# W3 and W_out by casting transfers from GpSimd, and a new order of the first steps, in a fused retention and FFN kernel

## The chip, the cores and the metric

The kernel runs on one core of a Trainium2 chip. The metric is the device time of one launch in microseconds (us). The profile gives one execution, in which the engines are called PE (TensorE, matmuls), PEld (its weight loads), DVE (VectorE), ACT (ScalarE), POOL (GpSimd) and SP (SyncE); the queues that issue transfers carry a q behind the name, so SPq is SyncE's queue. All transfers are carried out by the core's 16 DMA engines.

## What is computed

The reference first runs a retention recurrence for each batch and head and then a multiplicative FFN over all tokens:

```python
gamma = 1.0 - 2.0 ** (-5.0 - arange(8))
for t in range(768):                                  # q, k, v: 4 x 8 x 768 x 64
    state = gamma * state + outer(k[t], v[t])         # per batch and head, 64 x 64
    y[t] = q[t] @ state / sqrt(64)
x = y.transpose(0, 2, 1, 3).reshape(3072, 512)
a = x @ w1; b = x @ w2                                # w1, w2: 512 x 1024
out = ((a * b) @ w3) @ w_out                          # w3: 1024 x 1024, w_out: 1024 x 512
```

All inputs and the output are fp32 in DRAM. The kernel computes in fp16 with fp32 sums.

## The kernel before

The 3072 tokens are worked through as 12 tiles of 256, three for each batch. For one tile the steps are: load q, k, v (`load`, line 79), convert them to fp16 (`cast`, `cast_v`), turn q and k so that the head dimension lies on the partitions (`turn` and `turned`, or `dma_turn`), make masked scores (`scores`, `mask`), the tile's contribution to the state (`kv`, `state`), the part of the output that comes from the state and the part within the tile (`inter` in two parts, with `fence`, a small ACT copy, between them, then `av`), and write the result x as fp16 (`x_out`). Then follow the FFN's products with W1 and W2 and the product with the last matrix. For tiles 0 and 1 the W1 and W2 products go in steps of one 128-row block of a weight (`rows(W, tile, half, block)`, line 619 for the matmul), so that a step can start when its block is there. Later tiles use Strassen-like combinations of the weights (`combine`, `sums`, `prod`, line 867 for the matmul).

W3 and W_out are multiplied once, at the start: the product W3O = W3 W_out, 1024 x 512, takes the place of the two last matrices. W3 has eight blocks of 128 rows. For each block f the steps are: load it (`fetch('r5')` loads block 5 through `load_rows`, line 97, into an fp32 staging tile), convert it to fp16 (`cast_w3` or `cast_w3_half`, on DVE, ACT or POOL), turn it with eight 128x128 transposes on PE (`turn_w3`, matmul at line 260; half turns at line 249), copy the turned block from PSUM (`turned_w3`), and multiply it with the four parts of W_out (`w3_mm(f, i)`, four matmuls of 256 columns at line 280); when all four parts are done, `w3_out` copies the sum to SBUF. W_out comes in four parts of 256 rows (`fetch('wo2')` through `load_wo`, line 102), each converted by `cast_wo` (line 230). `fetch('w10')` loads block 0 of W1, `fetch('k0')` tile 0 of k.

Staging tiles are 16 in number (`NSTAGE`), 512 KB each, used in turn by all loads. All loads are issued by SP, in the order of the `fetch` lines, and in the trace their data come in that order. `warm(m)` runs m matmuls of 512 columns on zeros (line 796); they compute nothing that is used. POOL makes the constant tables: `identity()` (needed by the turns), `numbers`, `late_numbers`, `keeps` and `step_decays`.

The order of all steps is written out by hand as one long list, from line 948 to the end of the function; each engine works through its own instructions strictly in that order. Around the change the list reads, in the kernel before: loads of blocks 5, 2, 1, W_out 2, block 4, W_out 3, 0, 1, blocks 3, 6, 7, then tokens k0, q0, v0, block 0, tokens q1, k1, v1, then W1 and W2.

## Time and profile before

| | us |
|---|---|
| median of three runs (175.75 to 176.5) | 175.91 |
| the profiled execution, whole time | 176.04 |
| its span, first to last instruction | 174.2 |
| PE busy | 166.7 |
| PEld busy | 135.9 |
| DVE busy | 129.0 |
| ACT busy | 97.9 |
| POOL busy | 84.8 |

Queue q1, which holds all loads and stores of SP, carried 39.33 MB; 29.36 MB were read from DRAM and 6.29 MB written.

How to read the profile: a row of the timeline gives the start, the duration, the engine, the line of the kernel, the operation, output and input by the program's names with shape and type, how many instructions are merged into the row, and in brackets the idle time of the engine before it and what ended it. A row of the chain of waits gives the start, the length and what the time is put down to; the chain is followed back from the last instruction, at each step to what released it. PE's busy time is modelled, since matmuls are pipelined. Matmuls, copies and table work count as busy; issuing a transfer does not.

### The profile page before, as it was taken

Reading aid. Unit: us, or ns where it says so; the run is one execution under the profiler, and the core shown is the slowest. Engines: PE = TensorE matmul, PEld = TensorE weight load, DVE = VectorE, ACT = ScalarE, POOL = GpSimd, SP = SyncE. Lnnn points to the kernel's source line nnn. Section 1 sums busy time; section 2 is a strip of 40 time slices with the busy share of each in tenths; the row PEclk is TensorE's granted clock in tenths of the full one; section 3 lists DMA queues with packets and bytes.
Section 4 is the critical chain, followed back from the end, with each engine's and each line's share of the span. In section 5 each row is a group of like instructions: output and inputs, shape, how many; then the busy total and the mean of one; then the engine's idle time right before and its main releaser. Section 6 shows DMA issues by size and latency. Waiting matters only on the chain.

```text
span 174.2 us, 7288 instructions
## 1 busy us (share of the span) xinstructions
PE 166.7 (96%) x3196; PEld 135.9 (78%) x3196; DVE 129.0 (74%) x240; ACT 97.9 (56%) x169; POOL 84.8 (49%) x106
## 2 busy tenths in 40 slices
PE   6779999999999999999999999999999999999992
PEld 2349988778976799597899977959999598695972
DVE  0372469887865769979989698786998949686690
ACT  2055669688745596490653655637465483552732
POOL 1541841742899587496485966887312062000000
DMA  5999999999999999999978999999999999120033
GB/s 194 378 412 397 298 323 230 393 416 328 253 205 230 248 180 236 191 143 249 162 180 181 148 286 172 223 217 192 183 208 211 276 413 384 43 103 4 0 126 120
DMA packets 76160, 39.80 MB, mean 228 GB/s; under 512 B 53088, under 2 KB 71776, under 8 KB 76128
## 3 DMA queue, kind: packets, MB, share of 16 engines
q1 hardware_dynamic: 76128, 39.33, 92.8%
q8 instruction: 25, 0.41, 1.0%
q14 instruction: 7, 0.06, 0.1%
HBM read 29.36 MB, written 6.29 MB: 205 GB/s over the span
## 4 chain that ended last, share of the span: by engine, by line
PE 91%; DMA 3%; ACT 2%; SPq 0%; issue 0%; DVE 0%; ACTq 0%
PE psF L867 26%; PE psF L641 9%; PE psX L641 8%; PE psK L867 5%; PE psX L867 5%; PE psS L641 5%; PE psF L280 4%; DMA st<-in_moe_w_dram 3%; PE psF L619 3%; PE psX L509 3%; PE psX L280 2%; PE psS L619 2%; PE psF L653 2%; PE psX L535 2%; PE psS L396 2%; PE psK L619 1%
## 5 line engine op out<-in xcount | busy, mean ns | idle before, releaser
L867 PEld LDWEIGHTS <-wt 128*128 128x128 f16 x640 | 37.5, 98 | 0.5
L641 PEld LDWEIGHTS <-ht 128*128 128x128 f16 x224 | 21.0, 98 | 14.5 <-DVE ht L66 0.2
L867 PEld LDWEIGHTS <-w 128*128 128x128 f16 x480 | 28.8, 98 | 1.8
L63 ACT COPY u<-psF 128x512 f32<-128x512 f32 x32 | 18.4, 589 | 8.7 <-PE psF L867 6.4
L66 POOL TENSOR_TENSOR c<-u,p 128x512 f32<-128x512 f32 x12 | 15.2, 1276 | 11.7 <-ACT u L63 10.5
L867 PE MATMUL psF<-sodd,wt 128*128 128x128 f16 x240 | 18.1, 219 | 0.0
L641 PE MATMUL psF<-w3o,ht 128*128 128x256 f16 (+1 forms) x96 | 17.1, 326 | 0.0
L641 PE MATMUL psX<-w3o,ht 128*128 128x512 f16 (+1 forms) x80 | 15.2, 336 | 0.0
L66 DVE TENSOR_TENSOR ht<-psF,c 128x512 f16<-128x512 f32 x20 | 13.6, 687 | 0.9 <-POOL c L66 0.4
L619 PEld LDWEIGHTS <-w 128*128 128x128 f16 x128 | 12.3, 98 | 2.1 <-issue 0.4
L66 DVE TENSOR_TENSOR ht<-psX,c 128x512 f16<-128x512 f32 x19 | 12.8, 687 | 0.8 <-PE psX L867 0.4
L280 PEld LDWEIGHTS <-w3t 128*128 128x128 f16 x128 | 11.8, 98 | 2.1 <-DVE w3t L63 0.6
L66 POOL TENSOR_TENSOR v<-st,VN 128x1024 f16<-128x1024 f32 x6 | 11.4, 1902 | 1.3 <-DMA st<-in_v_dram 0.7
L874 ACT COPY psX<-psF 128x512 f32<-128x512 f32 x19 | 10.4, 576 | 2.4 <-issue 1.2
L413 DVE TENSOR_TENSOR am<-psS,keep 128x512 f16<-128x512 f32 x17 | 11.5, 684 | 0.3 <-PE psX L396 0.2
L867 PE MATMUL psX<-xt,w 128*128 128x128 f16 x152 | 11.6, 219 | 0.0
L867 PE MATMUL psF<-seven,wt 128*128 128x128 f16 x160 | 11.4, 219 | 0.0
L66 POOL TENSOR_TENSOR q<-st,QS 128x1024 f16<-128x1024 f32 x5 | 10.7, 2140 | 1.2 <-DMA st<-in_q_dram 1.2
L672 ACT ACTIVATE osb<-psF 128x512 f32<-128x512 f32 x8 | 4.8, 598 | 11.6 <-PE psF L641 11.6
L867 PE MATMUL psF<-xt,wt 128*128 128x128 f16 x160 | 11.1, 219 | 0.0
L867 PE MATMUL psF<-xt,w 128*128 128x128 f16 x160 | 11.1, 219 | 0.0
L66 DVE TENSOR_TENSOR c<-psK,u 128x512 f32<-128x512 f32 x10 | 6.9, 692 | 5.0 <-PE psK L867 4.4
(167 smaller groups left out, 375.0 us busy)
## 6 DMA issues: line engine op xcount, KB each, us to landing
st<-in_moe_w_dram SPq DMA_DIRECT2D x16, 512.0 KB, 7.9
st<-in_q_dram SPq DMA_DIRECT2D x12, 512.0 KB, 5.8
st<-in_v_dram SPq DMA_DIRECT2D x18, 256.0 KB, 5.9
st<-in_k_dram SPq DMA_DIRECT2D x18, 256.0 KB, 5.8
out_dram<-osb SPq DMA_DIRECT2D x9, 512.0 KB, 6.4
st<-in_moe_w_out_dram SPq DMA_DIRECT2D x4, 512.0 KB, 8.9
st<-in_k_dram SPq DMA_DIRECT2D x3, 512.0 KB, 10.8
st<-in_v_dram SPq DMA_DIRECT2D x3, 512.0 KB, 8.8
```

The lines of the kernel that those rows point to most:

```text
L63: {"v": nc.vector.tensor_copy, "g": nc.gpsimd.tensor_copy, "s": nc.scalar.copy}[eng](dst, src)
L66: (nc.vector if eng == "v" else nc.gpsimd).tensor_tensor(dst, a, b, op)
L280: nc.tensor.matmul(acc[f][:, cols], lhsT=w3t[f][:, g * 128 : (g + 1) * 128], rhs=WO[i][:, r, cols], start=(first and (r, c) == (0, 0)), st ...
L396: nc.tensor.matmul(ps[r][half(g), a, s, :], lhsT=kT[n][half(r), s, a, half(g)], rhs=qchunk(n, r, a, s, g), start=(a == 0 and s == 0), stop ...
L413: nc.vector.tensor_tensor(t[:, :, :, :].rearrange("p a s i -> p (a s) i"), ps[:, :, :, :].rearrange("p a s i -> p (a s) i"), keep64[:, :]. ...
L509: nc.tensor.matmul(dst, lhsT=TS[n, c][half(r), a, :], rhs=rhs, start=((g, o) not in begun), stop=False, skip_group_check=True,)
L535: nc.tensor.matmul(o, lhsT=v16[n][half(g), t, h * D : (h + 1) * D], rhs=rhs, start=((g, c) not in begun), stop=(n >= EO or t == 1), skip_g ...
L619: nc.tensor.matmul(rows_ps[w, n, uh][j // 2][:, j % 2, :], lhsT=W[d][:, f * 128 : (f + 1) * 128], rhs=XT[n][:, :, d, :], start=(first and ...
L641: nc.tensor.matmul(ps[:, x * w : (x + 1) * w], lhsT=HT[n][:, tb, f, :], rhs=W3O_all[:, f, c0 + x * w : c0 + (x + 1) * w], start=(f == 0 an ...
L672: nc.scalar.activation(o_tile(n, tb)[:, c0:c1], o_ps.pop((n, tb, c0, c1))[:, :], AF.Copy, scale=final_scale)
L867: nc.tensor.matmul(ps[:, j, :], lhsT=lhsT, rhs=rhs, start=(opens and j == 0 and c == 0), stop=(i in (2, 3, 4) and j == 3 and c == 1), skip ...
L874: nc.scalar.copy(WB[n, u, "C"][:, :, :], WB[n, u, "A"][:, :, :])
```

## The change

Seven row blocks of W3 (all but block 0) and all four parts of W_out no longer come through fp32 staging tiles and a conversion on an engine. GpSimd issues a transfer for each, from fp32 in DRAM straight into the fp16 tile (`gw3`, `gwo`), and the transfer converts. A new step `hold(f)` has SP issue a copy of 16 numbers out of the fp16 block f; SP waits for that block's transfer before it can issue this, and all token loads stand behind it in SP's list. Block 0 and W1 and W2 still come from SP into staging tiles and are converted on the engines (a function `gw` for W1 and W2 by casting transfer is added and is called nowhere).

The list of steps is written anew from its start to about line 1160 (tiles 0 to 2), and from there on steps are moved by one or a few places among their neighbours. Blocks are worked in the order 4, 1, 5, 2, 3, 7, 6, 0 by full turns; conversions of W1 and W2 go to other engines (POOL and DVE take more of them); the first W1 rows are those of block 2, and `fence(1)` stands ahead of the W1 conversions on ACT; the first loads after the tokens are W1 blocks 0, 2, 1, 3.

The diff up to the first W1 rows; the rest of it moves steps only.

```diff
@@ -186,6 +186,7 @@
     col_f = const.tile([128, 2, 128], FP, name="col_f")
     pos_f = const.tile([128, 2, 2, 64], FP, name="pos_f")
 
+    hold_t = const.tile([1, 16], HP, name="hold_t")
     W1 = [wpool.tile([128, DFF], HP, name=f"w1_{i}") for i in range(4)]
     W2 = [wpool.tile([128, DFF], HP, name=f"w2_{i}") for i in range(4)]
     WO = [wpool.tile([128, 2, DM], HP, name=f"wo_{i}") for i in range(4)]
@@ -226,6 +227,27 @@
 
     w3h, w3p, w3t, acc, w3n = {}, {}, {}, {}, {}
     w3h_tags = []
+
+    def gwo(i):
+        nc.gpsimd.dma_start(
+            WO[i][:, :, :], moe_w_out[i * 256 : (i + 1) * 256, :].rearrange("(p t) n -> p t n", t=2)
+        )
+
+    def gw3(f):
+        w3h[f] = att.tile([128, 1024], HP, tag="kq"[len(w3h_tags) % 2] + "16", name="w3h", bufs=3)
+        w3h_tags.append(f)
+        nc.gpsimd.dma_start(w3h[f][:, :], moe_w3[f * 128 : (f + 1) * 128, :])
+
+    def hold(f):
+        nc.sync.dma_start(hold_t[:, :], w3h[f][0:1, 0:16])
...
-    fetch('r5')
+    gw3(5)
+    warm(2, 'F2')
+    gw3(4)
+    gw3(1)
+    warm(3, 'F2')
+    gwo(3)
+    gwo(0)
     identity()
-    fetch('r2')
-    warm(2, 'F2')
-    fetch('r1')
+    step_decays()
+    gwo(2)
+    turn_w3(4, 'S0')
+    keeps()
+    warm(8, 'X1')
+    turned_w3(4, 's')
+    gw3(2)
+    gwo(1)
+    turn_w3(1, 'F0')
+    gw3(3)
+    turn_w3(5, 'K')
+    late_numbers()
+    turned_w3(1, 's')
     warm(3, 'F2')
-    fetch('wo2')
-    fetch('r4')
-    warm(8, 'X1')
-    fetch('wo3')
-    cast_w3(5, 'v')
-    fetch('wo0')
-    cast_w3(2, 'g')
-    fetch('wo1')
+    warm(4, 'F2')
+    turned_w3(5, 's')
+    gw3(7)
     numbers()
-    cast_w3_half(1, 0, 'v')
-    turn_w3(5, 'K')
-    cast_w3_half(1, 1, 'v')
-    turn_w3_half(1, 0, 'F0')
-    turn_w3_half(1, 1, 'S0')
-    fetch('r3')
+    w3_mm(4, 3)
+    w3_mm(4, 0)
+    w3_mm(4, 2)
+    w3_mm(5, 0)
+    gw3(6)
+    w3_mm(1, 2)
     turn_w3(2, 'F1')
-    cast_wo(2, 'v')
-    warm(3, 'F2')
-    turned_w3(2, 's')
-    fetch('r6')
-    late_numbers()
+    w3_mm(5, 2)
+    turned_w3(2, 'v')
+    w3_mm(5, 3)
+    w3_mm(2, 3)
+    hold(3)
+    w3_mm(1, 0)
+    turn_w3(3, 'S1')
+    fetch('k0')
+    w3_mm(2, 0)
+    fetch('q0')
+    turned_w3(3, 'v')
+    w3_mm(2, 1)
+    fetch('v0')
+    w3_mm(1, 1)
+    fetch('r0')
+    w3_mm(3, 2)
+    fetch('q1')
+    w3_mm(1, 3)
+    turn_w3(7, 'S1')
+    w3_out(1, 's')
+    turn_w3(6, 'F1')
+    w3_mm(3, 1)
+    turned_w3(6, 's')
+    w3_mm(4, 1)
+    fetch('k1')
+    cast('k', 0, 'v')
+    w3_mm(5, 1)
+    w3_mm(6, 3)
+    w3_out(5, 'v')
+    w3_mm(6, 1)
     arguments()
-    cast_w3_half(4, 1, 's')
-    turned_w3_half(1, 1, 'v')
-    turn_w3_half(4, 1, 'S0')
-    cast_w3_half(4, 0, 'v')
-    fetch('r7')
+    w3_mm(3, 3)
+    fetch('v1')
+    w3_out(4, 'v')
+    cast('q', 0, 's')
+    turn('k', 0, 'F1')
     w3_mm(2, 2)
-    turned_w3(5, 'v')
-    cast_wo(3, 's')
-    warm(4, 'F2')
-    turned_w3_half(4, 1, 'v')
-    turned_w3_half(1, 0, 'v')
-    fetch('k0')
-    w3_mm(5, 3)
-    turn_w3_half(4, 0, 'K')
-    w3_mm(4, 3)
-    turned_w3_half(4, 0, 's')
-    w3_mm(4, 2)
-    fetch('q0')
-    cast_wo(1, 'v')
-    w3_mm(1, 2)
-    w3_mm(5, 2)
-    cast_wo(0, 'v')
-    w3_mm(5, 1)
-    fetch('v0')
-    cast_w3(3, 's')
-    w3_mm(1, 3)
-    w3_mm(4, 0)
+    turned('k', 0, 'v')
+    w3_mm(3, 0)
     tables()
-    fetch('r0')
-    w3_mm(1, 0)
-    cast_w3(6, 'g')
-    w3_mm(5, 0)
-    turn_w3(3, 'S1')
-    fetch('q1')
-    step_decays()
-    w3_mm(2, 0)
-    turned_w3(3, 'v')
-    turn_w3(6, 'F1')
-    w3_mm(4, 1)
-    turned_w3(6, 's')
-    w3_mm(3, 3)
-    cast_w3(7, 'g')
-    w3_out(4, 'v')
-    w3_mm(1, 1)
-    fetch('k1')
-    w3_mm(2, 1)
-    keeps()
-    w3_out(1, 'v')
-    cast('k', 0, 's')
-    turn_w3(7, 'S1')
-    w3_mm(3, 0)
-    turn('k', 0, 'F1')
-    fetch('v1')
+    turned_w3(7, 'v')
     w3_mm(6, 0)
-    turned('k', 0, 'v')
-    cast('q', 0, 's')
-    w3_mm(6, 2)
-    turned_w3(7, 'v')
-    w3_mm(6, 3)
-    w3_mm(2, 3)
-    w3_out(5, 'v')
     fetch('w10')
+    cast_v(0, 'g')
     turn('q', 0, 'F1')
-    cast_v(0, 'g')
-    w3_mm(3, 2)
-    turned('q', 0, 's')
-    w3_mm(3, 1)
-    fetch('w11')
-    w3_mm(6, 1)
-    w3_out(3, 'v')
+    w3_mm(7, 1)
+    turned('q', 0, 'v')
+    w3_mm(7, 3)
+    fetch('w12')
     cast_w3(0, 's')
     scores(0, ('K', 'F1'), 0)
+    w3_mm(7, 2)
+    mask(0, 0, 0)
+    w3_out(2, 's')
     scores(0, ('S0', 'S1'), 1)
-    mask(0, 0, 0)
-    w3_mm(7, 1)
-    w3_out(6, 's')
-    w3_mm(7, 3)
+    mask(0, 1, 0)
+    w3_mm(7, 0)
+    w3_out(3, 's')
+    fetch('w11')
+    w3_mm(6, 2)
     mask(0, 0, 1)
-    w3_out(2, 's')
-    fetch('w13')
+    cast('q', 1, 's')
     kv(0, ('F0', 'K'))
-    cast('q', 1, 's')
     mask(0, 1, 1)
     turn_w3(0, 'S0')
+    w3_out(6, 's')
     state(0, 1)
-    w3_mm(7, 0)
+    fetch('w13')
     turned_w3(0, 's')
-    mask(0, 1, 0)
     inter(0, 0, ('F0', 'X1'))
-    fetch('w12')
-    w3_mm(7, 2)
     cast('k', 1, 'v')
     turn('q', 1, 'F1')
-    w3_out(7, 's')
     state(0, 2)
     turn('k', 1, 'X0')
     fence(0)
     turned('q', 1, 's')
     state(0, 3)
-    w3_mm(0, 3)
-    turned('k', 1, 'v')
     inter(0, 1)
     av(0)
+    turned('k', 1, 'v')
+    w3_out(7, 's')
+    fetch('w21')
+    scores(1, ('S0', 'X0'), 1)
+    x_out(0, 1)
+    cast_v(1, 'g')
+    w3_mm(0, 2)
+    mask(1, 1, 1)
+    w3_mm(0, 0)
     fetch('w23')
-    cast_v(1, 'g')
-    scores(1, ('S0', 'X0'), 1)
     x_out(0, 0)
-    w3_mm(0, 2)
+    w3_mm(0, 3)
     w3_mm(0, 1)
-    fetch('w21')
-    x_out(0, 1)
-    cast_wc(W1, 'w1', 0, 1, 's')
+    mask(1, 0, 1)
+    kv(1, ('S1', 'X1'))
+    fetch('w22')
+    w3_out(0, 's')
     scores(1, ('F0', 'K'), 0)
-    mask(1, 1, 1)
-    cast_wc(W1, 'w1', 0, 0, 's')
-    kv(1, ('S1', 'X1'))
+    cast_wc(W1, 'w1', 2, 1, 'g')
+    state(1, 1)
+    inter(1, 0, ('S0', 'S1'))
     mask(1, 1, 0)
-    fetch('w22')
-    w3_mm(0, 0)
-    cast_wh(W1, 'w1', 1, 0, 'g')
+    cast_wc(W1, 'w1', 0, 1, 'g')
+    fence(1)
+    cast_wc(W1, 'w1', 2, 0, 's')
     fetch('w20')
-    mask(1, 0, 1)
+    mask(1, 0, 0)
+    rows(W1, 0, 1, 2)
+    cast_wh(W1, 'w1', 1, 1, 's')
+    cast_wh(W1, 'w1', 1, 0, 'v')
+    rows(W1, 0, 0, 2)
     rows(W1, 0, 1, 0)
-    w3_out(0, 's')
-    state(1, 1)
-    cast_wh(W1, 'w1', 1, 1, 's')
+    cast_wc(W1, 'w1', 0, 0, 'v')
+    inter(1, 1)
+    fetch('q2')
+    av(1)
+    cast_wh(W1, 'w1', 3, 0, 's')
+    cast_wh(W1, 'w1', 3, 1, 'g')
+    rows(W1, 0, 1, 1)
+    x_out(1, 0)
...
```

More of the change, by code (lines that the diff above doesn't have):

```diff
@@ new lines @@
+    rows(W1, 1, 1, 3)
+    cast_wc(W2, 'w2', 2, 0, 's')
+    cast_wh(W2, 'w2', 1, 1, 'v')
+    rows(W1, 1, 1, 2)
+    cast_wc(W2, 'w2', 0, 0, 's')
+    rows(W1, 1, 1, 0)
+    state(1, 2)
+    rows(W1, 1, 0, 0)
+    combine(3, 1)
+    cast_wc(W2, 'w2', 0, 1, 's')
+    rows(W2, 0, 0, 3)
+    state(1, 3, 'v')
+    rows(W2, 0, 0, 2)
+    combine(1, 1)
+    rows(W2, 0, 0, 1)
+    fetch('v3')
+    late_arguments()
+    rows(W2, 0, 1, 0)
+    cast('q', 2, 'g')
+    rows_out('a', 1, 0, 1, 'v')
+    rows(W2, 0, 0, 0)
@@ new lines @@
+    rows_out('a', 1, 0, 0, 'v')
+    rows(W2, 0, 1, 1)
+    rows(W2, 0, 1, 2)
+    rows_out('b', 0, 0, 0)
+    rows(W2, 0, 1, 3)
+    cast('k', 2, 's')
+    combine(1, 0)
+    rows(W2, 1, 0, 2)
+    rows(W2, 1, 0, 1)
+    rows_out('b', 0, 1, 1)
+    rows_out('a', 1, 1, 1)
+    rows(W2, 1, 0, 0)
+    rows_out('a', 1, 1, 0)
+    fetch('k4')
+    rows_out('b', 0, 0, 1)
+    turn('k', 2, 'F2')
+    cast_v(2, 'g')
+    late_tables()
+    rows(W2, 1, 1, 0)
+    rows(W2, 1, 0, 3)
+    fetch('q5')
+    rows(W2, 1, 1, 3)
@@ new lines @@
+    rows_out('b', 1, 0, 1)
+    rows(W2, 1, 1, 1)
+    fetch('q3')
+    rows_out('b', 0, 1, 0)
+    o_part(0, 1, 0, 'F0')
+    cast('k', 3, 'g')
+    combine(2, 1)
+    fetch('v4')
+    rows(W2, 1, 1, 2)
+    turn('q', 2, 'S0')
+    rows_out('b', 1, 1, 1)
+    o_part(0, 1, 1, 'S1')
+    turned('q', 2, 'v')
+    cast_v(3, 'g')
+    o_part(0, 0, 0, 'F1')
+    rows_out('b', 1, 0, 0)
+    o_copy(0, 1)
+    turned('k', 2, 's')
+    rows_out('b', 1, 1, 0)
+    o_part(0, 0, 1, 'X0')
+    combine(3, 0)
@@ L1378 @@
     seed(4, 1, 'X1')
-    load('k', 8)
     cast_v(6, 'v')
     prod(4, 0, 6)
-    cast('q', 7, 'g')
     keep_part(4, 1, 'p5')
@@ L1500 @@
     prod(6, 1, 1, 'F0')
-    load('q', 11)
+    cast('q', 9, 'g')
     keep_part(6, 0, 'p5', 'v')
-    cast('q', 9, 'g')
     prod(6, 1, 5, 'F2')
```

360 lines of the change are left out of this document (147 added, 213 removed).

## The prediction

> **What bounds the kernel now.** I read the page first, then the busy time by stretches, then the chain of waits, then the timeline of the first 36 us.
>
> ```profile
> span 174.2 us, 7288 instructions
> PE 166.7 (96%) x3196; PEld 135.9 (78%) x3196; DVE 129.0 (74%) x240; ACT 97.9 (56%) x169; POOL 84.8 (49%) x106
> ...
> DMA  5999999999999999999978999999999999120033
> GB/s 194 378 412 397 298 323 230 393 416 328 253 205 230 248 180 236 191 143 249 162 180 181 148 286 172 223 217 192 183 208 211 276 413 384 43 103 4 0 126 120
> ```
>
> TensorE (PE) is busy 96% of the span, so the time can fall only where it does not work at its pace. The DMA line says where that may be: the 16 DMA engines are full from the second slice on.
>
> ```profile
> 0.00:5.00 5.00, 3.69 (x9) 1.26 (x10) 0.61 (x2) 1.28 (x1) 0.70 (x6) 1.00 0.61 211
> 5.00:10.00 5.00, 3.70 (x33) 2.02 (x31) 1.99 (x6) 0.47 (x1) 3.62 (x22) 1.00 1.01 392
> 10.00:15.00 5.00, 3.88 (x34) 2.81 (x34) 3.25 (x9) 2.69 (x4) 0.78 (x5) 1.00 1.02 417
> 80.00:100.00 20.00, 20.00 (x432) 17.55 (x420) 17.62 (x34) 9.37 (x17) 13.74 (x12) 1.00 1.06 180
> ```
>
> The columns are the stretch, its length, then PE, PEld, DVE, ACT, POOL busy, the granted clock, the DMA share and GB/s. From 80 to 100 us PE never rests; in the first 15 us it rests 3.7 us and part of its work is only warming. The chain shows what it waits for:
>
> ```profile
> 1.73 6.06 DMA st<-in_moe_w_dram
> 7.81 0.44 DVE w3h L63
> ...
> 12.82 0.14 issue
> 12.96 0.60 PE psF L280 x4
> ...
> 16.40 0.44 PE psK L280 x4
> ...
> 17.71 0.45 PE psS L260 x8
> ...
> 33.30 0.56 PE psF L280 x4
> ...
> 33.88 0.59 ACT w3o L63
> 34.49 1.04 ACT w L63
> ...
> 35.76 0.31 PE psS L509 x8
> 36.07 0.45 PE psS L535 x32
> ```
>
> ```profile
> 34.05 0.38 PE L619 MATMUL psK<-xt,w 128*128 128x256 f16 x2 [0.21 <-DVE am L407]
> ...
> 35.04 0.31 PE L509 MATMUL psS<-qT,t 64*64 64x128 f16 x8
> 35.76 0.31 PE L509 MATMUL psS<-qT,t 64*64 64x128 f16 x8 [0.41 <-ACT fence L520]
> ```
>
> A W3 step (`w3_mm`, line 280) is worth 0.44 us of PE, a turn (line 260) 0.45. Before 12.96 PE has done three and a half turns and one step, 2.0 us of useful work; from 12.96 to 33.85 the chain holds nothing but PE. So useful work u = t - 10.95 in that stretch, and u = 22.9 at 33.85. Then 2.66 us go by up to 36.51. Of them two W1 row steps are work (0.87, the price of two W3 steps), and `inter(1, 0)` (0.25), and `inter(1, 1)` with av(1) (0.75, from 35.76 to 36.51); 0.8 us are waiting, most of it for the fence, which stands behind a W1 cast on ACT. So u = 24.77 at 36.51. Everything later is PE at its pace: **the question is when the changed kernel has u = 24.77**, and what it gains or loses by then stays to the end.
>
> **Loads.** SP's queue delivers in order; the first reader of a load that had to wait for it shows its landing.
>
> ```profile
> 0.81 1.34 SPq L99 DMA_DIRECT2D st<-in_moe_w_dram  x3
> 4.66 0.69 DVE L63 CAST w3h<-st 128x1024 f16<-128x1024 f32 x1 [3.46 <-DMA st<-in_moe_w_dram]
> 16.87 1.04 POOL L63 CAST w3h<-st 128x1024 f16<-128x1024 f32 x1 [5.96 <-DMA st<-in_moe_w_dram]
> 22.23 1.04 ACT L63 CAST q<-st 128x1024 f16<-128x1024 f32 x1 [1.20 <-DMA st<-in_q_dram]
> 24.17 1.93 POOL L66 TENSOR_TENSOR v<-st,VS 128x1024 f16<-128x1024 f32 x1 [2.36 <-DMA st<-in_v_dram]
> 32.51 1.14 ACT L63 CAST w<-st 128x512 f16<-128x512 f32 x2 [1.36 <-DMA st<-in_moe_w_dram]
> 33.87 1.03 POOL L63 CAST w<-st 64x1024 f16<-64x1024 f32 x1 [1.23 <-DMA st<-in_moe_w_dram]
> ```
>
> Row block 5 lands at 4.66, the tenth load (block 6) at 16.87: 1.36 us a weight load. Tokens q0 and v0 land 1.94 us apart. Twelve weight loads and six token loads after the first give 4.66 + 16.3 + 11.6 = 32.6, and the first W1 block does land at 32.51, the second 1.36 behind it. So the whole stretch is paced by transfers, and PE reaches W1 about when W1 arrives.
>
> **Part 1: eleven loads cast on the way.** It removes 11 conversions (0.69 on DVE, 1.04 on ACT or POOL, the rows above) between a landing and its use; all but the first few were hidden. The first conversion cost PE directly (the 0.44 us DVE piece of the chain). What a casting load costs, this trace does not show. It reads the same 512 KB and writes half. Bounds: 0.68 us if written bytes count (half of 1.36), 1.36 if it runs like the plain load, 1.94 if it runs like the token loads. I take 1.27, which is 512 KB at the 412 GB/s of the third slice: nearest is the plain load, with its write side relieved. It can also start later. GpSimd starts at 0.80 (its first row, in part 4), as SP does, and the delay lies between 0 and 1.04 us, one POOL copy; I take 0.5, about SP's own 0.45 for an issue (three in 1.34). The Trainium skill ("DMA: Bandwidth & Descriptors", Specifications) gives a first byte after about 1 us on GpSimd's path against 0.6 on SyncE's: by it the delay would be 0.4 and the end 0.1 us earlier; no row here shows it.
>
> With 1.27, load n lands at 5.16 + 1.27(n-1): block 4 at 6.4, W_out 3 at 9.0, W_out 0 at 10.2, W_out 2 at 11.5, block 2 at 12.8, block 3 at 15.3, block 7 at 16.6, block 6 at 17.9.
>
> **Part 2: the new order on PE.** The number of PE instructions is the same. The twenty warming matmuls stay, but fifteen now stand behind the first turn.
>
> ```profile
> 1.26 2.53 PE L796 MATMUL psF<-zeros 128*128 128x512 f16 x5 [1.26 <-DVE zeros L128]
> 3.58 2.97 PE L796 MATMUL psX<-zeros 128*128 128x512 f16 x8
> ...
> 11.95 0.88 PE psF L796 x4
> ```
>
> At full pace one costs 0.22 (four in 0.88). Turn 4 at 6.4, eight warmings (1.76), turns 1 and 5 (0.9), seven warmings (1.54): the first W3 step starts at 11.05. Five steps end at 13.25, block 2 is there, so u = 3 x 0.45 + 5 x 0.44 = 3.55 at 13.25: u = t - 9.7, which is 1.25 us ahead of before. Four steps, turn 3 at 15.45 (landed 15.3), five steps, turns 7 and 6 at 18.1 and 18.55 (landed 16.6, 17.9): no wait.
>
> **Part 3: SP waits (`hold(3)`).** Queued behind it on SP are all token loads, block 0, and then W1 and W2. It opens at 15.3, when two casting loads, 2.5 us of work for the DMA engines, are still to come. The first load of before landed 3.4 us after its issue ended (4.66 less 0.81 + 0.45), 2.0 of it latency ahead of 1.36 of transfer; the two loads cover that latency, so I cost the wait at nothing. If GpSimd has not issued them by then, the cover is gone and everything on SP comes up to 2.0 us later. The second W1 block, which the changed order uses first, lands at 5.16 + 10 x 1.27 + 3 x 1.36 + 6 x 1.94 = 33.6, and with half a POOL cast (0.52) PE may start the W1 rows at 34.1. PE gets there with u = 23.15 (`inter(1, 0)` now comes first), without waits at 32.85. So W1's arrival decides: the lead of 1.25 us is lost again by waiting. The fence no longer stands behind a W1 cast, so its wait is not paid again: two rows, `inter(1, 1)` and av(1) later u = 24.77, at 34.1 + 1.62 = 35.72 instead of 36.51. **Gain 0.79 us.**
>
> **Part 4: GpSimd's own work.** It now issues 11 loads between its tables. From the starts and ends of the rows below, identity is 0.57, the step decays 1.43, the mask 1.5, late numbers 1.6 (9.30 to 10.91), numbers 2.4 (6.91 to 9.30): 7.5 us ahead of the last load.
>
> ```profile
> 0.80 0.20 POOL masks.py:197 MEMSET ident<- 128x128 f16 x1 [0.29 <-POOLq L1838]
> ...
> 1.08 0.29 POOL masks.py:199 TENSOR_SCALAR_AFFINE_SELECT ident<-ident 128x128 f16<-128x128 f16 x1
> ...
> 6.91 0.14 POOL L141 IOTA key_i<- 128x16 int32 x1
> ...
> 9.30 0.60 POOL L164 IOTA tok_i<- 128x16 int32 x1
> ...
> 10.38 0.53 POOL L173 TENSOR_SCALAR_AFFINE_SELECT keep<-keep 64x64 f32<-64x64 f32 x2
> 17.84 1.43 POOL L214 MEMSET GS<- 64x64 f32 x8
> ...
> 20.31 0.32 POOL L153 MEMSET keep<- 128x256 f32 x1
> 20.69 1.12 POOL L157 TENSOR_SCALAR_AFFINE_SELECT keep<-keep 64x128 f32<-64x128 f32 x4
> ```
>
> The price of one issue on GpSimd is not in this trace: at least SP's 0.45, at most perhaps 1.5 (between a POOL copy's 1.04 and its two-input operation's 1.93). I take 0.6, nearest to the issue on SP. Block 6 then lands at 0.8 + 7.5 + 11 x 0.6 + 3.4 = 18.3, a little behind the transfers' own 17.9 and still ahead of turn 6 at 18.55.
>
> The reordering behind 60 us moves steps among each other where PE is already full (the 80 to 100 row); nothing on the path, give or take 0.3. The sum is against the profiled execution, 176.04 (span 174.2 and 1.84 around it); the median of the three runs is 175.91, 0.13 lower. 175.91 - 0.79 gives **175.1**. About 0.5% (0.88 us) is what a measurement of this kernel can tell from no change.
>
> **Rivals.**
> (B, slower) GpSimd's issue becomes the bound, at `turn_w3(6)`: block 6 lands at 11.7 + 11p for a price p. Turn 6 wants it at 18.55, and PE has 1.25 us in hand before W1, so the price bites from p = 0.74. At p = 1.0 block 6 lands at 22.7, 4.15 late and 2.9 beyond the reserve: 175.1 + 2.9 = 178.0; from 0.88 on (1.6 beyond) it is slower by over 0.5%. For it: numbers and mask stand ahead of the last loads on GpSimd. Against: SP's 0.45.
> (C) PE's pace. The first warmings start about 0.46 apart (five from 1.26 to 3.58), the late ones 0.22, though the granted clock reads 1.00 in that stretch. If PE falls back to 0.46 while it waits for block 4, the eight warmings cost 3.7 and turn 4 costs 0.9: the first step starts at 13.4, u = t - 12.05, W1 rows at 35.2, 1.1 later than in the sum: 176.2. For it: an idle stretch from 3.6 to 6.4. Against: the four at 11.95 run at 0.22 after the rests of the first 15 us. The Trainium skill ("TensorE: Matmul & The Clock Gate", Part 1) has the array start at half rate and need a busy window of about 3.4 us; that would be this case.
> (D) The casting load is paid by written bytes, 0.68: W1 is there before 29, and PE alone decides. Turn 4 at 5.85, first step at 10.5, u = t - 9.15, u = 24.77 at 33.92, 2.6 early: 173.3. For it: 417 GB/s is flat over a whole stretch, like a limit; which side sets it, no row says.
> (E) It costs 1.94: W1's second block lands 6.7 later than in the sum, 5.9 us lost net: 181.8.
> (F) The change does nothing for time: the loads run at 1.36. W1's second block lands at 34.5, rows start at 35.0, u = 24.77 at 36.6: 176.0. The DMA share of 1.01 from 5 to 10 us speaks for it, and so does the mask on DVE for which the first W1 row waited at 34.05: that work stays. The Trainium skill ("DMA: Bandwidth & Descriptors", Issuing engines are not separate DMA queues) says that a second issuing engine brings no bandwidth, which is this case.
>
> **How the numbers follow.** Forecast 0.36 (its own range 174.3 to 176.0, from delays of 0 to 1 us and loads of 1.2 to 1.36), B 0.20, C 0.07, D 0.18, E 0.08, F 0.11. Faster by over 0.5%: D and 0.20 of the forecast, 0.38; slower: B and E, 0.28; within: the rest, 0.34. The range 173.0 to 178.0 takes in all but E, the dearer end of B (0.08) and the cheaper end of D (0.05).
>
> **What would show it.** Right: GpSimd's issues under 0.74 us each; eleven casting loads about 1.27 apart; first W3 step near 11; PE's last long wait at the W1 rows near 34, av(1) done near 35.7. Wrong: a PE wait at `turn_w3(6)` (B), warmings 0.46 apart after 6 us (C), W1 landing before 30 (D) or after 36 (E), W1 rows at 35 (F).

## The result and the profile after

| | before | after |
|---|---|---|
| median of the runs, us | 176.2 (175.75 to 179.86, 4 runs) | 182.29 (181.72 to 184.39, 4 runs) |
| ratio to before, 95% interval | | 1.0376 [1.0265, 1.0488] |
| profiled execution, us | 176.04 | 181.78 |
| its span, us | 174.2 | 180.1 |
| VectorE busy, 41 to 61 us of the span | 15.06 | 18.36 |

The change makes the kernel slower by 6 us; the forecast was 175.1. A median, here and below, is over all executions and a ratio is made from the undisturbed ones alone, so where the runs of a kernel spread widely the two differ, and it is the ratio that counts.

The page of the changed kernel, the lines that answer to those of before:

```profile
span 180.1 us, 7275 instructions
PE 168.5 (94%) x3196; PEld 136.7 (76%) x3196; DVE 129.4 (72%) x237; ACT 91.2 (51%) x163; POOL 84.9 (47%) x111
...
DMA  3999999999999998699995999989999999030033
GB/s 54 198 201 186 238 324 304 403 407 320 240 225 269 246 247 186 62 143 211 218 194 107 179 272 130 264 167 195 207 201 189 275 410 354 11 120 4 0 122 117
```

and its stretches:

```profile
0.00:5.00 5.00, 2.47 (x5) 0.53 (x5) 0.27 (x1) 1.28 (x1) 3.78 (x13) 1.00 0.39 70
5.00:10.00 5.00, 3.30 (x14) 1.74 (x15) 0.00 (x0) 1.01 (x1) 4.55 (x18) 1.00 1.08 197
10.00:15.00 5.00, 4.94 (x43) 3.44 (x42) 0.00 (x0) 1.93 (x2) 3.46 (x25) 1.00 1.11 205
15.00:20.00 5.00, 5.00 (x55) 4.41 (x54) 1.38 (x2) 0.00 (x0) 0.00 (x0) 1.00 0.83 161
80.00:100.00 20.00, 19.49 (x473) 16.83 (x470) 18.01 (x34) 8.42 (x17) 12.17 (x12) 1.00 1.11 189
```

While the casting loads run, the DMA engines are as full as before (share 1.08 and 1.11), but they write half the bytes (197 and 205 GB/s where before wrote 392 and 417). So a casting load keeps the DMA engines about as long as a plain one. From 15 to 20 us the share falls to 0.83: for a while the engines have too little to do. And from 80 to 100 us PE rests for half a microsecond, where it never rested.

To see where the 5.9 us of span went, one can follow a step that both kernels make once in each tile. The first half of `o_unit(n, 0)`, the product with W3O, is such a step; here are its starts for n = 2, 4 and 5 in the chain of waits, first of the kernel before, then of the changed one (start, length, what):

```profile
69.87 1.83 PE psF L641 x8
...
92.02 1.75 PE psF L641 x16
...
103.06 1.73 PE psF L641 x8
```

```profile
72.36 1.83 PE psF L663 x8
...
95.30 1.75 PE psF L663 x16
...
108.76 1.73 PE psF L663 x8
```

The lateness is 2.49, 3.28 and 5.70 us, and it stays at 5.7 to the end. So there are at least two losses: 2.5 us are lost before 72 us, and 3.2 us between there and 109 us, where the forecast had "nothing on the path". The list of PE's waits names what stood there (the first row is the wait for the first casting load, the other two lie between 92 and 108 us):

```profile
PE psS L282 <- DMA w3h<-in_moe_w_dram: 2.9, 1, 2.9
PE psK L465 <- POOL v L66: 2.1, 1, 2.1
...
PE psS L418 <- issue: 0.5, 1, 0.5
```

**First 40 us.** The chain of the changed kernel in this stretch, up to the first W1 rows:

```profile
9.18 6.93 DMA w3h<-in_moe_w_dram
...
16.12 0.61 SPq L242
...
20.18 6.85 DMA st<-in_moe_w_dram
...
27.11 1.04 ACT w3h L63
...
29.01 1.06 ACT q L63
...
36.06 0.61 DVE am L429
...
36.71 0.38 PE psK L641 x2
```

It runs from the casting load of block 3 over the hold (L242) and three token issues to the load of block 0, which lands at 27.05. `cast_w3(0)` stands on ACT in front of two `w3_out`, the cast of q1 and one more `w3_out`, so all these stood behind that load. ACT itself waited only 0.25 us for it, but 1.61 us for q0, which landed at 24.00: the whole stream of loads behind the hold is late. PE, in the end, waits 0.4 us for a bank that ACT empties, and 0.3 us for the mask on DVE ahead of the first W1 rows. The W1 block that these rows need comes hardly sooner: it landed at 35.67, and the first half of its cast on GpSimd was done at about 36.25.

```profile
35.67 1.17 POOL L63 CAST w<-st 128x512 f16<-128x512 f32 x2 [1.25 <-DMA st<-in_moe_w_dram]
```

Where the kernel before was at av(1)'s end at 36.51, the changed one has it at 39.04 (with one row step of 0.44 more done): 2.1 us late.

**40 to 64 us.** VectorE is busy 18.36 of 20 us from 41 to 61. Two things put it there: it casts three half blocks of W2, and one of its products of fp16 weights takes longer. In this execution the stretch costs little: e5 below, which has only the new first part, comes to `o_unit(2, 0)` at 72.15, 0.2 us earlier. The products of two weight blocks (`wt<-w,w`) on VectorE between 40 and 62 us, in the kernel before and in the changed one (name, count, shortest, median and longest in ns):

```profile
L66 DVE TENSOR_TENSOR wt<-w,w x3: 685/686/693, 41.1 to 44.1; 128x1024 f16<-128x1024 f16 x3
```

```profile
L66 DVE TENSOR_TENSOR wt<-w,w x4: 678/684/1636, 44.3 to 56.2; 128x1024 f16<-128x1024 f16 x4
```

**95 to 110 us.** On GpSimd the cast of k tile 8 stands in front of the cast of v tile 7, before and after:

```profile
97.51 1.04 POOL L63 CAST k<-st 128x1024 f16<-128x1024 f32 x1
...
99.20 1.90 POOL L66 TENSOR_TENSOR v<-st,VN 128x1024 f16<-128x1024 f32 x1
```

```profile
102.92 1.04 POOL L63 CAST k<-st 128x1024 f16<-128x1024 f32 x1 [2.20 <-DMA st<-in_k_dram]
...
104.61 2.35 POOL L66 TENSOR_TENSOR v<-st,VN 128x1024 f16<-128x1024 f32 x1
```

After the change GpSimd waits 2.20 us for k tile 8. The diff moves `load('k', 8)` from behind `seed(4, 1)` to behind `state(6, 1)`, that is, on SP's queue behind `dma_turn('k', 7)`, a transposing transfer that can be issued only when k tile 7 has been cast. `kv(7)` on PE then waits 2.1 us for v.

### The profile page after: what moved, and what is told of

Same layout as the page of the kernel before. It is cut to its first block, busy times and chain, and to the rows that moved or that the text cites. A ratio compares the mean times of both kernels' runs of the same rounds, so it can differ in the third digit from the quotient of the medians.

```text
span 180.1 us, 7275 instructions
## 1 busy us (share of the span) xinstructions
PE 168.5 (94%) x3196; PEld 136.7 (76%) x3196; DVE 129.4 (72%) x237; ACT 91.2 (51%) x163; POOL 84.9 (47%) x111
## 4 chain that ended last, share of the span: by engine, by line
PE 73%; DMA 8%; POOL 6%; DVE 6%; SPq 2%; issue 2%; ACT 2%; DVEq 0%; ACTq 0%; POOLq 0%
PE psF L889 24%; PE psF L663 9%; PE psX L663 8%; PE psK L889 5%; PE psS L663 5%; PE psX L889 4%; DMA w3h<-in_moe_w_dram 4%; DMA st<-in_moe_w_dram 4%; PE psX L531 2%; PE psF L675 2%; PE psX L557 2%; SPq L86 2%; PE psS L418 2%; PE psF L641 1%; POOL v L66 1%
## 5 line engine op out<-in xcount | busy, mean ns | idle before, releaser
L63 ACT COPY u<-psF 128x512 f32<-128x512 f32 x33 | 19.0, 588 | 10.5 <-PE psF L889 7.9
L66 POOL TENSOR_TENSOR v<-st,VS 128x1024 f16<-128x1024 f32 x3 | 6.3, 2094 | 13.3 <-DMA st<-in_v_dram 13.3
L66 POOL TENSOR_TENSOR v<-st,VN 128x1024 f16<-128x1024 f32 x6 | 12.1, 2009 | 0.8 <-DMA st<-in_v_dram 0.8
L63 DVE COPY w3t<-psF 128x1024 f16<-128x1024 f16 x1 | 0.7, 691 | 14.8 <-PE psF L282 14.8
```

Source lines behind the costliest of these rows:

```text
L63: {"v": nc.vector.tensor_copy, "g": nc.gpsimd.tensor_copy, "s": nc.scalar.copy}[eng](dst, src)
L66: (nc.vector if eng == "v" else nc.gpsimd).tensor_tensor(dst, a, b, op)
```

## The experiments

The first theories, from the two traces: H, the hand-over leaves the DMA engines empty and that is the loss of the start; W, the casting loads themselves are; S, the hold is a mistake as such; Q, the late k load is the loss of the end, against L, another late thing takes its place. After four kernels they made way for T, three separate losses (transfers at the start, VectorE from 41 to 63 us, the late k load), with rivals that name one of them alone.

Unless said, a kernel is the changed one with the edit shown. "Before" is the median of the kernel before, measured beside it.

### The hold

**e1.** The hold goes to block 2, and SP's queue opens 2.7 us earlier (at 13.45):

```diff
     gw3(2)
+    hold(2)
     gwo(1)
...
-    hold(3)
```

> SyncE's first transfer waits for block 2 (the seventh casting load) in place of block 3 (the ninth); all else as changed. Theory H (the wait leaves the DMA engines empty between the last casting loads and the first token data, 2.2 us at 17 to 19 us, and every later load comes that much late): the empty stretch is gone, the W1 rows start about 2 us earlier than 36.7, and the time falls by 1.5 to 2.2, to about 180. Rival W (it is the casting loads themselves, their price or their start, that make W1 late): the DMA engines have the same work to do, tokens only take from the last casting loads, and the time stays at 181.5 to 182.5.

182.71 us (181.47 to 183.83), before 176.41, ratio 1.0339 [1.0236, 1.0442]. The hole closes, the time does not follow: theory H fell. This execution came to `o_unit(2, 0)` even later than the changed kernel's, at 74.11 (e4 below: 72.60).

**e2.** No hold at all: `-    hold(3)`.

> The wait is taken out: SyncE issues tokens from 0.8 us on, beside GpSimd's casting loads. Theory H, with transfers of two queues sharing the engines by time: W3 lands at about half its rate, the first W3 step comes some 5 us later than at 13.2, block 6 lands after 25, PE starves on W3; 184 or more. Rival S (the wait protects nothing; a casting load's long rows take their turn among the tokens' short ones and lose little): W3 lands at most 20% later, the supply as a whole starts 2 us earlier, and the time falls by 2 us or more, to 180 or less.

189.34 us (186.96 to 191.58), ratio 1.0639 [1.0511, 1.0767]. Token loads and casting loads share the DMA engines from the start, and PE waits up to 5.6 us for one W3 block. With this order of loads the hold is needed; it isn't a mistake in itself.

### The late k load

**e3.** `load('k', 8)` back to its old place:

```diff
     seed(4, 1, 'X1')
+    load('k', 8)
     cast_v(6, 'v')
...
     state(6, 1)
-    load('k', 8)
```

> One step is put back to its place in the kernel before: the load of k for tile 8 stands again ahead of the transposing transfer of k for tile 7 in SyncE's list. Theory Q (the second loss, 2.4 us at 102 to 107 us, comes from that load's being issued behind the transposing transfer: GpSimd stands 2.2 us at the conversion of k8, its conversion of v7 comes late, PE waits 2.1 for it): that wait goes and the time falls by 2.0 to 2.5, to about 179.5. Rival L (tile 8 is late because everything is late since the start, and some other load will be last): under 0.5 gained, 181.3 or more.

181.65 us (179.69 to 182.06), ratio 1.0262 [1.0173, 1.0351], 1.1% below the changed kernel's. The wait ahead of `kv(7)` is gone, and tile 4 to tile 5 takes 11.0 us as before (13.5 in the changed kernel). But this execution reached `o_unit(2, 0)` at 75.34, 3.0 us later than the changed kernel's, with the same code up to there. One microsecond of that was there at av(1)'s end already (40.04 against 39.04); the other two were the first sign of the loss on VectorE:

```profile
L66 DVE TENSOR_TENSOR wt<-w,w x4: 680/1282/2421, 45.3 to 58.5; 128x1024 f16<-128x1024 f16 x4
L66 DVE TENSOR_TENSOR wt<-w,wt x1: 1860/1860/1860, 54.3 to 54.3; 128x1024 f16<-128x1024 f16 x1
```

The first row holds the four instructions of the row above, the second one more product (0.68 us in the changed kernel's execution). Of the five, three now took 1.86 to 2.42 us. The rows beside two of them say why. VectorE, then GpSimd, in e3:

```profile
49.72 1.88 DVE L66 TENSOR_TENSOR wt<-w,w 128x1024 f16<-128x1024 f16 x1
...
54.30 1.86 DVE L66 TENSOR_TENSOR wt<-w,wt 128x1024 f16<-128x1024 f16 x1
```

```profile
49.12 1.93 POOL L66 TENSOR_TENSOR v<-st,VS 128x1024 f16<-128x1024 f32 x1 [2.29 <-DMA st<-in_v_dram]
...
53.72 1.90 POOL L66 TENSOR_TENSOR v<-st,VN 128x1024 f16<-128x1024 f32 x1 [1.22 <-DMA st<-in_v_dram]
```

GpSimd's operations end at 51.05 and 55.62, VectorE's products at 51.60 and 56.16: 0.55 and 0.54 later. They started while GpSimd was at work, and did nearly all of their own 0.68 us only when it was done.

**e4.** e1 and e3 together.

> The edits of the first and the third run together. Theories H and Q: the two losses lie in different stretches and add up, so about 4 us come back: 177.5 to 178.3. If the two are one loss (Rival L), no more than the larger of the two alone.

180.51 us (179.67 to 181.29), ratio 1.0219 [1.0141, 1.0296]. The two repairs bring back a third of the loss (two fifths by the ratios), half of what was expected.

### Which part of the list: three cuts

There are two places, at `av(0)` (about 31 us) and ahead of `turn('q', 4)` (about 68 us), at which both lists have done the same steps (at the first but for one W3 step, which was added or left out, and the order of the four W1 loads). So the new list can be put together with the old one.

**e5.** The changed kernel up to the first place, then the old list: `after[: av(0)] + before[av(0) :]`.

> The changed kernel's first part (up to the last step before av(0)), then every step of the kernel before in its old order; only the order in which the four W1 blocks are fetched is the old one too. Theory T (three separate losses): the changed kernel has its av(1) done 2.1 us late (transfers), loses 0 to 3 us more between 41 and 63 us, where VectorE is busy all the time, and 3.2 us from tile 5 on (GpSimd's casts of the ninth k tile and v tile 7). Here only the first is left: 176.4 + 2.1 = 178.5, VectorE with idle time again in 50 to 60 us, no wait of kv(7). Rival Y (it is the transfers that set it all, the late start is carried on and grows): 181 to 182.

178.98 us (178.56 to 179.47), before 176.31, ratio 1.0166 [1.0101, 1.0230]. As theory T said.

**e6.** The reverse: `before[: av(0)] + after[av(0) :]`.

> The other half alone: the first part of the kernel before (plain loads on SP, conversions on the engines), then from av(0) on the changed kernel's order of steps, with its order of the four W1 fetches. T: the transfers' loss is gone, VectorE's and the late k load's stay: 176.4 + 0 to 3 + 3 = 179 to 182, with kv(7) waiting about 2 us for a GpSimd cast. Y: no slower than 176.9.

183.35 us (181.08 to 184.53), ratio 1.0320 [1.0226, 1.0414]. PE waits 2.5 us ahead of `kv(7)`, 0.9 and 0.7 us for VectorE and 0.5 us at scores(6). There is no casting load in this kernel, and yet it loses nearly as much as the whole change: rival Y fell.

**e10.** Only the middle is new: `before[: av(0)] + after[av(0) : turn('q', 4)] + before[turn('q', 4) :]`.

> The kernel before up to av(0), then the changed kernel's order up to turn('q', 4), then the old order again. T: VectorE has three W2 half-block casts more (2.0 us) and its fp16 products of the weight blocks (0.69 us each in the kernel before) take up to 2.4 us where they start beside a GpSimd operation; 176.3 + 1.5 to 4 = 178 to 180. Rival (TensorE at its pace, as in the kernel before): 176.3.

178.64 us (176.47 to 180.56, ten runs), before 175.93 (175.37 to 177.06, 19 runs), ratio 1.0082 [1.0041, 1.0122]. By the ratio that is 1.4 us, just short of T's range; the runs spread over 4 us, where those of before have 1.7. The profiled execution was a short one (176.85), and in it only one of the five products was long (1.64 us).

Five profiled executions have the new order of the middle, and they show what the collisions with GpSimd cost. The table adds up by how much VectorE's operations between SBUF tiles lasted longer between 40 and 63 us than they do alone (in e3 by 0.84 for a product of the state and by 1.20, 1.18 and 1.74 for three weight products), and gives the time from av(1)'s end to `o_unit(2, 0)`:

| execution | longer by, us | av(1)'s end to `o_unit(2, 0)`, us |
|---|---|---|
| the changed kernel | 1.8 | 33.3 |
| e10 | 1.8 | 33.2 |
| e4 | 2.7 | 34.1 |
| e1 | 4.4 | 34.7 |
| e3 | 5.0 | 35.3 |

The more time VectorE lost to GpSimd, the later the kernel, by about 0.6 us for each.

**e9.** Only the end is new: `before[: turn('q', 4)] + after[turn('q', 4) :]`.

> The kernel before up to turn('q', 4), about 68 us, and from there on the order of the changed kernel (both have done the same steps by then). Theory T: 176.3 + 2.4 for kv(7), which waits for GpSimd's cast of v tile 7 behind the ninth k tile's late load, + 0.5 for the stop ahead of scores(6) = 179.2. Rival (those waits are only the echo of the lateness of what ran before): 176.3.

179.87 us (178.97 to 180.78), ratio 1.0201 [1.0151, 1.0250]. `kv(7)` waits 2.1 us, the stop at scores(6) is 0.5: the rival fell. Another 1.1 us is a wait for a fence at 71 us, and that one comes from the cut: ACT has the cast of q5 in front of `fence(3)`, and q5 lands at 69.97 in this mixture. The changed kernel doesn't have this wait.

**e15.** e9 with the edit of e3.

> e9 with the load of the ninth k tile back at its old place, ahead of the transposing transfer of k tile 7 on SyncE's queue. T: the wait of 2.1 us ahead of kv(7) goes: 179.9 - 2.1 = 177.8; what is left against the kernel before (1.5 to 2) is the waits for the fence (1.1) and the stop of 0.5. Rival (the wait only moves to the next late thing): no more than 0.5 gained.

178.61 us (177.38 to 180.47), before 176.13, ratio 1.0108 [1.0032, 1.0184]. By the ratios that is 0.93% less than e9, 1.6 us; the intervals overlap, but the wait of 2.1 us is gone from the list of waits, and those of 1.2 and 0.5 are what is left. The wait did not move on.

### The first part: transfers or order

**e7.** e5 with the hold on block 2.

> e5 with SyncE's queue let go by block 2 in place of block 3 (the hole of the DMA engines closed). T: av(1) is done 0.5 us earlier than in e5 (38.54 against 39.04 in the two kernels that tried it with the new order), so 178.0; Y: no smaller than e5.

179.82 us (179.39 to 179.90), ratio 1.0199 [1.0147, 1.0251]: not better than e5, perhaps worse. The hole at 17 to 19 us is closed, but a new one opens at 28 to 30 us (DMA share 0.60; why, no run shows). T's half microsecond did not come.

**e12.** The transfers alone, in the order of the kernel before:

```diff
-    fetch('r5')
+    gw3(5)
...
-    cast_w3(5, 'v')
...
+    hold(3)
     fetch('k0')
```

and the same for blocks 1, 2, 3, 4, 6, 7 and W_out.

> Every step in the order of the kernel before, but the seven W3 blocks and W_out as fp16 by casting transfers from GpSimd, the conversions of these eleven gone, and SyncE's queue let go by block 3. Theory T (a casting load takes as long as a plain one, and the queue's hand-over leaves the DMA engines idle for about 2 us): W1 comes 1 to 2.5 us later, 177.3 to 178.8. Rival G (the conversions were worth something, and the loss of the first part is its new order): 175.5 to 176.3.

179.84 us (178.47 to 180.64), before 175.93, ratio 1.0173 [1.0110, 1.0236]: rival G fell, and the loss is a little larger than T's range. The chain goes through the hold here too, and the hole is deeper (share 0.35 and 0.57; 1.07 and 1.18 in the two microseconds ahead of it and behind it). The chain, then the two stretches of the hole:

```profile
8.46 8.97 DMA w3h<-in_moe_w_dram
...
17.44 0.63 SPq L242
...
18.14 5.23 DMA st<-in_k_dram
```

```profile
18.00:20.00 2.00, 2.00 (x22) 1.80 (x20) 0.00 (x0) 0.52 (x2) 0.00 (x0) 1.00 0.35 63
20.00:22.00 2.00, 2.00 (x29) 1.88 (x27) 0.87 (x2) 0.62 (x1) 0.00 (x0) 1.00 0.57 159
```

Whatever the removal of eleven conversions brought, it is less than what the transfers with the hold cost.

**e14.** The order alone: e5 with `fetch` in place of `gw3` and `gwo`, the conversions back (eight on DVE, two on ACT, one on GpSimd), and no hold.

> e5 without the transfers' change: the new order of the first steps, but W3 and W_out by plain loads on SyncE in the new order of blocks and converted by VectorE, ScalarE and GpSimd; no hold; then the old order from av(0) on. Theory T (the first part lost its time by the transfers: a start 0.5 us later on GpSimd and the hand-over's hole): W1 lands as in the kernel before, 32.5 and 33.9, and the time is 175.5 to 176.5. Rival O (the new order itself is late): 177.5 to 179, as e5.

178.76 us (177.44 to 181.31, 11 runs), before 176.13, ratio 1.0107 [1.0072, 1.0143]. T's 175.5 to 176.5 was not reached: as it stands, the new order costs time with plain loads as well.

**e17.** e14 with one step moved:

```diff
-    turn_w3(4, 'S0')
     keeps()
     warm(8, 'X1')
+    turn_w3(4, 'S0')
```

> e14 with the eight warmings ahead of the first turn, as in the kernel before, so that TensorE doesn't rest from 3.6 to 6.7 us. Theory (the matmuls behind that rest ran 0.43 us apart, twice the later price): first W3 step about 1.5 us earlier, near 11.7, and since W1 lands at 33.9 at the latest use, 0.3 to 0.8 us less than e14. Rival: W1's arrival decides, no difference from e14.

176.73 us (176.03 to 177.68, 12 runs), ratio 1.0027 [1.0002, 1.0053]: 0.8% less than e14, or 1.4 us, more than expected. That was the reason: in e14 PE rested from 3.8 us until block 4 was there, and its next eight warmings ran 0.45 us apart. PE's rows of e14:

```profile
6.64 1.03 PE L282 MATMUL psS<-ident,w3h 128*128 128x128 f16 x8 [2.86 <-DVE w3h L63]
7.46 3.62 PE L818 MATMUL psX<-zeros 128*128 128x512 f16 x8
```

The profiled execution of e17 shows about half of the gain: its first W3 step starts at 13.03, where e14's starts at 13.68 and 11.7 was expected. It is the longest of the twelve (177.68); PE rested 1.84 us in it ahead of the second turn, and the granted clock then read 0.50 from 9 to 12 us.

With plain loads and the pace repaired, the new order of the first part is nearly as good as the old one (0.3% slower), and no better.

**e18, e19.** Does the pace matter in the changed kernel too? e18 is e5 with the edit of e17, and e19 is e5 once more on the same chip.

> e5 with the eight warmings ahead of the first turn (the edit of e17). Theory R (in the changed first part the chain runs from the casting load of block 3 over the hold to the load of block 0, 27.1, and from its cast over ScalarE's queue to the banks that inter(0, 0) needs; TensorE's first steps have slack): within 0.4 us of e5. Rival P (the pace decides here too): 0.7 to 2.0 us less than e5.

> The same kernel as e5, unchanged, for comparison on the same chip: 178.98, give or take 0.5.

179.16 us (178.29 to 179.98) against 179.70 (178.06 to 179.90), before 175.96; ratios 1.0186 [1.0150, 1.0223] and 1.0190 [1.0155, 1.0224]. No difference that can be told, as theory R said, although the first W3 step starts 2.3 us earlier (13.50 in e5). PE's row of e18, and its chain:

```profile
11.22 1.73 PE L302 MATMUL psK<-wo,w3t 128*128 128x256 f16 x12
```

```profile
16.11 0.63 SPq L242
...
19.85 7.10 DMA st<-in_moe_w_dram
...
27.03 1.04 ACT w3h L63
```

The hold and the landing of block 0 come within two tenths of a microsecond of where e5 has them (16.15 and 27.13), and `o_unit(2, 0)` starts at 72.19 (72.15 in e5). PE gained 2.3 us there and gave all of it back waiting. PE's slack is small, though: in e19's execution the first W3 step started at 14.27, its chain runs over PE from there to av(1), which ends 0.7 us later than in e5. So the two paths are about equally long, and shortening one of them alone gains next to nothing.

e18 and e17 differ in the transfers alone: casting loads with the hold in the one, plain loads with conversions in the other. 1.0186 against 1.0027 is 1.6%, or 2.8 us. That is the price of the transfers and the hold in the first part, so T was right about them, and wrong in that the order had a price of its own.

### The middle: VectorE

**e8.** e4 with the three W2 casts moved to ScalarE (`cast_wh(W2, 'w2', 1, 0, 'v')` to `'s'`, and the same for `3, 0` and `1, 1`).

> e4 (hold on block 2, k load at its old place) with the three half-block casts of W2 that run on VectorE given to ScalarE, which is busy 2.0 of 5 us from 50 to 55. T: VectorE is the bound from 41 to 63 us, and is relieved of 3 x 0.67 us there: 180.5 - 1 to 2 = 178.5 to 179.5, o_unit(2,0) earlier by that than in e4. Rival P (TensorE is at its pace there in any case, busy 5.00 of 5 us): as e4, 180.5.

184.74 us (184.65 to 184.81), ratio 1.0483 [1.0431, 1.0535]: 4 us worse than e4. ACT has the room, but not at that place in its order. ACT's row and VectorE's row of e8:

```profile
44.54 4.56 ACT L63 CAST w<-st 128x512 f16<-128x512 f32 x6
```

```profile
48.02 1.81 DVE L66 TENSOR_TENSOR wt<-w,w 128x1024 f16<-128x1024 f16 x1 [4.87 <-issue]
```

VectorE's first product there (`combine(3, 1)`, W2 block 3 less block 1) needs the three casts that were moved (and one on GpSimd); the last of them stands fourth in ACT's row of six. Everything on VectorE stood behind that product for 4.87 us.

**e16.** e10 with W2's blocks 1 and 3 by casting transfers from GpSimd, so that no engine casts them:

```diff
-    fetch('w21')
+    gw('w2', 1)
...
-    cast_wh(W2, 'w2', 1, 0, 'v')
```

and the same for block 3 and the other three casts.

> e10 with W2's blocks 1 and 3 loaded as fp16 from GpSimd at the places where SyncE fetched them, so that three half-block casts (0.69 us each) leave VectorE and one (1.04) leaves GpSimd. Theory D (VectorE is the bound from 41 to 60 us): median 178.6 - 1 to 2.1 = 176.5 to 177.6. Rival (TensorE's own pace there): 178.6 as before. Rival Q (the transfers from GpSimd's queue push SyncE's back at that place): over 179.

177.87 us (176.67 to 179.96, nine runs) against 178.64 for e10; ratios 1.0077 [1.0040, 1.0115] and 1.0082 [1.0041, 1.0122]. VectorE's busy time from 41 to 61 us falls from 18.58 to 17.21 us, the time by less than can be told. That the added casts don't matter isn't shown by this: in the new kernel two of the added issues (1.22 us) stand on GpSimd in front of the cast of v1, and `kv(1)` waits 0.9 us for it, so the edit brought a wait of its own.

**e13.** The kernel before, with three copies more on GpSimd that nobody reads:

```diff
     cast_wh(W1, 'w1', 3, 0, 'g')
+    for _ in range(3):
+        copy('g', spare[:, :], W1[0][:, :])
```

> The kernel before with three more copies of a finished fp16 block (128x1024) on GpSimd, where it is idle (from 40.6 us on, up to its own product at 44.4); nothing reads them. Four of VectorE's fp16 products run there, 0.69 us each. Theory C (VectorE's products of fp16 SBUF tiles and GpSimd's operations can't run together): the products that start beside a copy last until about 0.6 us after its end, up to 1.6 us each; the end 0 to 2 us later. Rival N (no such conflict): they stay at 0.69 and the end at 176.3.

176.98 us (176.09 to 179.33, ten runs), ratio 1.0044 [1.0019, 1.0070]; the profiled execution is the longest of the ten. The copies ran earlier than planned, beside other VectorE work, and what they met is telling. VectorE's rows, then GpSimd's:

```profile
36.57 1.18 DVE L63 CAST w<-st 128x512 f16<-128x512 f32 x1 [1.23 <-DMA st<-in_moe_w_dram]
37.67 0.41 DVE L66 TENSOR_TENSOR s<-psX,t 128x256 f32<-128x256 f32 x1
38.00 1.27 DVE L552 TENSOR_TENSOR xt<-psS,YS 128x512 f16<-128x512 f32 x2
39.20 0.57 DVE L66 TENSOR_TENSOR vn_x<-tok_i,LGH 128x16 f32<-128x16 int32 x1
```

```profile
36.43 3.31 POOL L63 COPY spare<-w 128x1024 f16<-128x1024 f16 x3
```

The cast, from SBUF to SBUF, takes 1.18 us instead of 0.43, and the small product `vn_x` of two SBUF tiles 0.57 instead of 0.17. The two operations between them read PSUM and take what they took in the kernel before (0.42, and 1.28 for two), with GpSimd's copies running beside them all the time. So theory C holds, with a narrower condition: it is VectorE's work between SBUF tiles that waits. The Trainium skill ("SBUF — State Buffer", SBUF: two separate sides) has this as an exclusive lock: GpSimd shares one pair of ports with VectorE's operations that run in a two-port mode or have both inputs in SBUF; whoever starts first holds it for the whole instruction, and the other waits. The rows here agree, and GpSimd loses by it as well (the cast of v tile 7 after the change, 2.35 us instead of 1.90).

## Why the prediction was wrong

**What bounds the kernel.** Right for the kernel before. Wrong was the step from there, "Everything later is PE at its pace", carried over to a new list: PE at 96% has no slack to show, but the engines that feed it had, and the new list used it up.

**Price of a casting load, 1.27.** Too low. Block 4 starts its turn at 6.70, block 3 is seen at 16.12 by SP, seven loads later: 1.35 each, the plain load's 1.36. That is rival F's price, and e12 shows its consequence: with nothing gained per load, only costs are left. (412 GB/s, from which 1.27 was taken, was read in a slice in which plain loads took 1.36.)

**GpSimd's issues, 0.6.** Right; rival B fell:

```profile
1.31 1.78 POOL L239 DMA_DIRECT2D w3h<-in_moe_w_dram  x3 [0.80 <-POOLq L1844]
3.07 1.07 POOL L232 DMA_DIRECT2D wo<-in_moe_w_out_dram  x2
```

0.53 to 0.59 each, the first 0.5 us after SP's first of before, as assumed.

**First W3 step at 11.05.** Wrong: 13.19. Rival C, given 0.07, is what happened; the eight warmings behind the early turn took 3.2 us instead of 1.76:

```profile
7.52 3.21 PE L818 MATMUL psX<-zeros 128*128 128x512 f16 x8
...
13.19 1.47 PE L302 MATMUL psK<-wo,w3t 128*128 128x256 f16 x12
```

By e18 this miss cost next to nothing in this kernel, since the loads were as late as PE; by e14 and e17 the same edit is worth 1.4 us with plain loads.

**Part 3, the hold "costed at nothing".** This is the first step that failed. The two casting loads behind block 3 were to cover the hand-over, and they were already issued, as assumed. But the prediction set them against the latency of 2.0 us alone. SP sees the block at 16.12 and is done issuing the hold and k0 only at 17.55; the latency comes on top of that, and the DMA share from 18 to 20 us is 0.61. By the prediction's own terms block 0 lands at 25.04 (5.16 + 10 x 1.27 + 3 x 1.94 + 1.36). It landed at 27.05, 2.0 us late, and the W1 block that it put at 33.6 landed at 35.67, 2.1 us late. Block 3 was 0.8 us late already (16.12 instead of 15.3), from the price of the loads and their start; the rest, an estimate of 1.2 us from these figures, goes to the two loads behind it and the hand-over. The prediction also did not ask who stands behind q0 and block 0 on ACT. The transfers with the hold cost 2.7 us (e5), 3.7 in the repeat (e19), 2.8 by e18 against e17. How much of this a better hand-over would bring back is not settled: closing the hole gained nothing in e1 and e7, and perhaps 1.1 us in e4 (against e3).

**"The reordering behind 60 us: nothing on the path, give or take 0.3".** This is the second step that failed. It took PE's full 80 to 100 us as proof that its neighbours may be moved, and did not count, for each moved step, which queues it is moved past. `load('k', 8)` was moved behind a transposing transfer on SP's queue, and 2.1 us of PE's time went there (e3, e9, e15). Together with the next stretch this is the larger part of the loss (e6: 3.2%, e5: 1.7%).

**The stretch from 36 to 60 us** had no term at all. There the new list puts VectorE's weight products where GpSimd is at work. The loss differs from execution to execution: e10 is 1.4 us slower by its ratio, with single runs from half a microsecond on. It grows with the time that VectorE's operations lose beside GpSimd (the table under e10). That the collisions make the whole of it is argued from that and from the rows of e3 and e13; no kernel was run with the collisions alone removed, and the longest runs of e10 have no trace.

By the ratios the three losses are 1.7% (e5), 0.8% (e10) and 0.9% (the late k load, e9 against e15), together 3.4%, against 3.8% measured: within the intervals they add up to the whole. Not explained is the stop of 0.5 us at scores(6). No kernel here beat the kernel before.

## What to carry to other kernels

When an engine sits at 96%, as PE did here, a new order has little to gain and much to lose: go through the moved steps queue by queue, and ask for each load, cast and product what now stands in front of it and who waits behind it. A casting transfer saved an engine's conversion here and nothing of the transfer's time (1.35 us against 1.36), so look for it to pay where conversions are the bound. When a queue is held back until another queue's load has landed, count the issues as well as the latency: two loads of cover were too few here, four closed the hole (e1, e7), though without a gain that could be told. Products between SBUF tiles on VectorE belong where GpSimd is idle.

## What the runs showed of the hardware

- A load of 512 KB that converts to fp16 on the way takes 1.35 us in a row of such loads, as long as one that writes all 512 KB.
- VectorE's operations between SBUF tiles wait for a GpSimd operation that started before them: the same fp16 product took 0.68 us alone and up to 2.42 us beside one (e3); operations that read PSUM were not touched (e13).
- TensorE started at half pace and kept it over a rest of 2.9 us: the first five warmings took 2.53 us, and the eight behind the rest took 3.2 to 3.6 us (the changed kernel, e14), where at the later 0.22 each they would take 1.76. The column of the granted clock read 1.00 all that time. The Trainium skill ("TensorE: Matmul & The Clock Gate", Part 1) has a busy window of about 3.4 us before full rate; the full pace is reached here some 4 us after the first turn, at about 10.6.
- The same column did show a fall from full pace: in e17 at the end of a rest of 1.84 us, and in e12 a little after one of 3.57 us, the granted clock went to 0.50 for 3.4 us (added up from windows of 1 us), and the turns behind the rest in e17 took 1.04 us instead of 0.62.
- Without the hold, token loads from SP and casting loads from GpSimd ran at once, and PE waited 5.6 us for one W3 block (e2).
